# Pooled attention and two MLPs on one core: queries and keys handed over dimension first

## Chip, cores and metric

One core of a Trainium2 chip runs the whole program. The metric is the device time in microseconds from launch to end; the kernel before has a median of 672.22 us over three runs (671.64 to 672.84).

## What is computed

The inputs q, k and v have shape (2, 8, 1152, 64): 2 batches, 8 heads, 1152 positions, 64 dimensions, in float32. Queries are averaged two by two, so that each head has 576 pooled queries.

```python
q_pool = q.reshape(B, H, S // 2, 2, D).mean(axis=3)
scores = scale * np.matmul(q_pool, k.transpose(0, 1, 3, 2))
scores = scores - np.max(scores, axis=-1, keepdims=True)
attn = np.exp(scores)
attn = attn / (np.sum(attn, axis=-1, keepdims=True) + 1e-09)
x = np.matmul(attn, v)
```

The result, as 1152 rows of 512, goes through two MLPs of width 2048: `leaky(x @ w_in) @ w_out`, then the same with silu.

## The kernel before, in words

`attention()` (L287) works on 8 pairs of heads, `mlps()` (L908) follows with no attention work left. Only the attention changes.

TensorE multiplies in the type fp32r, which keeps fewer bits than float32. So every query and key operand is split into a high part (the value copied to fp32r) and a low part (value minus high part). Per pair and head j the kernel holds `K2` (128 x 1152): the 64 dimensions of the high part on one half of the partitions and those of the low part on the other half; `QH` (128 x 576): the high part of the queries on both halves; `QL` (low part of the queries, plus one row with the negated row maximum); and `KA` (high part of the keys, plus rows of ones, which adds that maximum to the product).

A pair goes through these steps.

- **Load** (`load_kq`, L358): keys and queries come from memory with positions on the partitions: one DMA for both heads' keys, three for the queries, for pair 0 by head. All DMAs are issued by SyncE, on one queue and in the order of the program (L347).
- **Pool** (`pool_q`, L408): GpSimd adds the even and the odd queries, three instructions for a pair.
- **Prepare** (`prep`, L448): TensorE turns 128 x 128 blocks by a matmul with an identity (L435), into PSUM banks. ScalarE copies from there to the high parts (L352), VectorE subtracts to get the low parts of the keys (L531) and queries (L492), and the bank is free when all have read it. For a pair after the first that is 4 groups with 15 transposes in all, which hold one bank each. In pair 0 some low parts go by way of a staging tile to GpSimd (L502, L525). `copy_qh` copies QH to the other half by DMA, `copy_ka` (L554) fills KA from K2 by four DMAs.
- **Maxima** (`max_tile`, L562): for each of 9 blocks of queries and 3 chunks of 384 keys, one matmul (L580, L581, L584) into a bank and one VectorE maximum over it (L588). `finish_max` (L599) reduces the three and SyncE writes the negated maxima as a row into QL by small DMAs (L347, `ql<-mn`, ten for a pair).
- **Scores** (`scores`, L622): for each of 9 key blocks, head and half of the queries, two matmuls (L638) into a bank and an exponential on ScalarE into a tile `e` (L642). Ten `e` tiles go round.
- **Values and sums**: `pv` (L664) multiplies `e` by v into two banks of their own (L670), and `sum_up` (L652) adds the `e` tiles up on GpSimd (L659), 16 instructions for a pair; VectorE does it for the last pair. `sums` and `finish` (L691, L768) get the reciprocals by way of DMAs and scale the values on VectorE (L773, L777).

Six PSUM banks serve preparation, maxima and scores in turn; the tokens of L319 count them. The order of instructions on every engine is written out by `Plan` (L188): each task has an engine, an estimated duration, a due time and the tasks it follows, and the planner starts on each engine the ready task that is due first. The due times of pair p are `T0 + (p + x) * T`, with T0 = 18 and T = 30 and an x for each step from `PARAMS` (L47): loads at -1.7, preparation at -1.4 to -1.15, maxima from -0.97 to -0.2. The durations of the plan set the order alone; on the chip every engine runs its list in that order, waiting at semaphores.

In the last four pairs the first weights are loaded and unpacked as well (`weight_steps`, L869): eight pieces on ScalarE and VectorE, and of the first four pieces the low parts on GpSimd (L170).

Of the kernel before, what the change touches and what calls it, by code (L numbers as in the profile page):

```python
# [11 lines left out]
ALU = mybir.AluOpType  # L12
# [7 lines left out]
def pooled_attention_two_mlps(  # L20
# [12 lines left out]
    B, H, S, D = q.shape  # L33
# [253 lines left out]
def attention(ctx, tc, q, k, v, xh, xl, weights, end_p):  # L287

    nc = tc.nc
    B, H, S, D = q.shape  # L290
# [24 lines left out]
    ps_v = ctx.enter_context(tc.tile_pool(name="ps_v", bufs=1, space=PSUM))  # L315
# [3 lines left out]
    plan.tokens(bank=NBANK, qnat=1, knat=2, vnat=2, q2=1, ops=3, acc=2, pvs=1, v=1, r=1, raw=3, wt=P["wt"])  # L319
    plan.ring("e", NE)  # L320
    banks = list(range(NBANK))

    def bank(name):
        i = banks.pop(0)
        return ps_b.tile([128, 512], F32, tag=f"b{i}", name=name), i
# [4 lines left out]
    KE = NKT // 2 * 128  # L330

    ident = const.tile([128, 128], F32, name="ident")
# [9 lines left out]
    knat, qnat, vnat, q2, K2, QH, mx, acc, e_t, vps, pvs, rec, box = ({} for _ in range(13))  # L342
# [14 lines left out]

    def load_kq(p, due, begin):  # L358
        b, h0 = p // HP, 2 * (p % HP)

        def k_part(j):
            def go():
                if p not in knat:
                    knat[p] = nat.tile([128, 2, NKT, D], F32, tag="knat", name="knat")
                js = slice(0, 2) if j is None else slice(j, j + 1)
                hs = slice(h0 + js.start, h0 + js.stop)
                return knat[p][:, js], k[b, hs].rearrange("j (p t) d -> p j t d", p=128)
            return go

        def q_part(j):  # L370
            def go():
                if p not in qnat:
                    qnat[p] = nat.tile([128, 2, 2 * (NFULL + 1), D], F32, tag="qnat", name="qnat", bufs=1)
                t = qnat[p]
                if j == 2:
                    return t[0:HALF, :, 2 * NFULL:, :], q[b, h0:h0 + 2, 2 * NFC:, :].rearrange("j (p r) d -> p j r d", p=HALF)
                return (
                    t[:, j, 0:2 * NFULL, :].rearrange("p (t r) d -> p t (r d)", r=2),
                    q[b, h0 + j, 0:2 * NFC, :].rearrange("(t p r) d -> p t (r d)", p=128, r=2),
                )  # L380
            return go

        made = {}
        if p == 0:
            made["k", 0] = dma(due, k_part(0), take=("knat",), lag=2.5)
            made["q", 0] = dma(due, q_part(0), order=[made["k", 0]], take=("qnat",), lag=2.5)
            made["q", 2] = dma(due, q_part(2), order=[made["q", 0]], lag=2.5)
            made["k", 1] = dma(due, k_part(1), order=[made["q", 2]], lag=3.0, begin=3.0)
            made["q", 1] = dma(due, q_part(1), order=[made["k", 1]], lag=3.0, begin=3.5)
        else:  # L390
            made["k", 0] = made["k", 1] = dma(due, k_part(None), take=("knat",), lag=5.0, begin=begin)
            made["q", 0] = dma(due + 0.1, q_part(0), take=("qnat",), lag=5.0, begin=begin)
            made["q", 1] = dma(due + 0.1, q_part(1), order=[made["q", 0]], lag=5.0)
            made["q", 2] = dma(due + 0.1, q_part(2), order=[made["q", 1]], lag=5.0)
        return made
# [12 lines left out]
    def pool_q(p, loads, due):  # L408
        def tail():
            q2[p] = nat.tile([128, NFULL + 1, 2, D], F32, tag="q2", name="q2", bufs=1)  # L410
# [841 lines left out]
```

## Time and profile before

| | us |
|---|---|
| median of three runs | 672.22 |
| the profiled execution | 673.36 |
| its span, first to last instruction | 670.6 |
| TensorE busy | 653.0 (97%) |
| VectorE busy | 456.1 (68%) |
| GpSimd busy | 385.3 (57%) |
| ScalarE busy | 322.7 (48%) |

The profiled execution takes 2.8 us more than its span. Busy times are sums of the durations of instructions; matmuls overlap one another, so TensorE's share says only that it seldom stood still. In the rows below PE is TensorE, PEld its weight load, DVE is VectorE, ACT ScalarE, POOL GpSimd, SPq the queue of SyncE.

### The profile page before, as it was taken

How to read it: one execution, taken by the hardware profiler on the slowest of the kernel's cores; microseconds unless marked ns; L12 is line 12 of the kernel's file. 1: busy time of each engine (PE TensorE's matmuls, PEld its weight loads, DVE VectorE, ACT ScalarE, POOL GpSimd, SP SyncE). 2: the span in 40 equal slices, each digit the busy share in tenths (PEclk: the TensorE clock that was granted, in tenths of full speed). 3: DMA queues.
4: the chain of work that ended last, by engine and by line, in shares of the span. 5: the costliest groups of instructions: out<-in, count | busy, mean ns of one | idle time of the engine just before them, and what ended most of it. 6: DMA issues, size and time to landing. Idle time of an engine off the chain costs nothing.

```text
span 670.6 us, 10322 instructions
## 1 busy us (share of the span) xinstructions
PE 653.0 (97%) x3741; PEld 530.1 (79%) x3741; DVE 456.1 (68%) x700; ACT 322.7 (48%) x694; POOL 385.3 (57%) x294
## 2 busy tenths in 40 slices
PE   6899999998999999999999999999999999999997
PEld 4566677675666666888988988999988888888986
DVE  6776768586878775885576676698988888522222
ACT  5446566584857466554443343345446543322110
POOL 7576978878797851665354354376756454522120
PEclk9799999998999999999999999999999999999999
DMA  5555151537364320033222232222233322000012
GB/s 143 142 102 146 37 142 38 143 92 199 80 193 99 104 64 20 31 127 95 95 94 95 95 95 94 95 69 89 94 95 109 111 95 95 0 1 1 1 47 94
DMA packets 41897, 59.71 MB, mean 89 GB/s; under 512 B 15324, under 2 KB 24568, under 8 KB 41848
## 3 DMA queue, kind: packets, MB, share of 16 engines
q1 hardware_dynamic: 41848, 59.07, 30.4%
q8 instruction: 29, 0.48, 0.3%
q14 instruction: 20, 0.16, 0.1%
HBM read 49.81 MB, written 2.42 MB: 78 GB/s over the span
## 4 chain that ended last, share of the span: by engine, by line
PE 87%; DVE 6%; DMA 3%; ACT 1%; issue 1%; SPq 1%; POOL 0%; DVEq 0%; ACTq 0%
PE ph L1046 30%; PE po L1117 15%; PE pf L1166 15%; PE pss L638 10%; PE pv L670 10%; PE pmx L584 4%; DVE mx L588 3%; PE prep L435 2%; DMA d<-sum 1%; DVE ql L492 1%; DMA r<-d 1%; DMA cmp<-d 1%; DMA qnat<-in_q_dram 1%; ACT qh L352 1%; SPq L347 1%
## 5 line engine op out<-in xcount | busy, mean ns | idle before, releaser
L1099 POOL TENSOR_TENSOR gl<-a,gh 128x512 fp32r<-128x512 f32 (+1 forms) x64 | 97.2, 1519 | 142.7 <-ACT gh L1093 76.1
L659 POOL TENSOR_TENSOR acc<-acc,e 128x576 f32<-128x576 f32 x98 | 140.3, 1452 | 31.0 <-ACT e L642 29.6
L642 ACT ACTIVATE e<-pss 128x288 f32<-128x288 f32 x288 | 101.4, 411 | 80.1 <-PE pss L638 73.2
L588 DVE TENSOR_REDUCE mx<-pmx 128x1 f32<-128x384 f32 x216 | 110.9, 551 | 34.4 <-PE pmx L584 29.0
L1046 PE MATMUL ph<-xh,w0h 128*128 128x320 f32 (+1 forms) x384 | 109.0, 338 | 0.5 <-ACT pvs L684 0.5
L1046 PE MATMUL ph<-xh,w0l 128*128 128x320 f32 (+1 forms) x384 | 108.7, 337 | 0.0
L1046 PE MATMUL ph<-xl,w0h 128*128 128x320 f32 (+1 forms) x384 | 108.6, 337 | 0.0
L638 PE MATMUL pss<-qh,k 128*128 128x288 f32 x288 | 88.1, 322 | 3.9 <-DVE mx L588 3.8
L670 PE MATMUL pv<-e,vnat 128*64 128x288 f32 x576 | 86.5, 422 | 0.0
L638 PE MATMUL pss<-ql,ka 128*128 128x288 f32 x288 | 81.4, 298 | 0.9 <-DMA ql<-mn 0.9
L638 PEld LDWEIGHTS pss<-qh,k 128*128 128x128 f32 x288 | 55.0, 191 | 25.2 <-DVE mx L588 10.8
L135 DVE TENSOR_SCALAR wt<-wt 128x512 f32<-128x512 f32 x56 | 40.4, 722 | 49.6 <-ACT wt L131 49.6
L1046 PEld LDWEIGHTS ph<-xh,w0h 128*128 128x128 f32 x384 | 67.7, 188 | 8.2 <-ACT pvs L684 1.0
L1046 PEld LDWEIGHTS ph<-xh,w0l 128*128 128x128 f32 x384 | 66.9, 188 | 5.6
L1046 PEld LDWEIGHTS ph<-xl,w0h 128*128 128x128 f32 x384 | 66.9, 188 | 5.0
L584 PE MATMUL pmx<-k,qh 128*128 128x384 f32 x192 | 65.4, 385 | 2.1 <-ACT e L642 1.0
L170 POOL TENSOR_TENSOR w1l<-wt,w1h 128x512 fp32r<-128x512 f32 x32 | 44.4, 1397 | 39.8 <-ACT w1h L166 39.8
L139 DVE TENSOR_SCALAR wt<-wt 128x512 uint32<-128x512 uint32 x56 | 57.9, 1033 | 1.7
L170 POOL TENSOR_TENSOR w0l<-wt,w0h 128x512 fp32r<-128x512 f32 x32 | 44.7, 1397 | 24.7 <-ACT w0h L166 24.7
L670 PEld LDWEIGHTS pv<-e,vnat 128*64 128x64 f32 x576 | 35.4, 137 | 28.9 <-issue 13.5
L1166 PE MATMUL pf<-w1h,gl 128*128 128x512 f32 x144 | 56.2, 390 | 0.0
L1166 PE MATMUL pf<-w1l,gh 128*128 128x512 f32 x144 | 56.1, 390 | 0.0
(85 smaller groups left out, 1127.6 us busy)
## 6 DMA issues: line engine op xcount, KB each, us to landing
wraw<-in_moe_w_in_dram SPq DMA_DIRECT2D x32, 512.0 KB, 3.6
wraw<-in_moe_w_out_dram SPq DMA_DIRECT2D x32, 512.0 KB, 3.1
vnat<-in_v_dram SPq DMA_DIRECT2D x8, 576.0 KB, 5.5
qnat<-in_q_dram SPq DMA_DIRECT2D x16, 256.0 KB, 5.1
knat<-in_k_dram SPq DMA_DIRECT2D x7, 576.0 KB, 5.3
ka<-k SPq DMA_DIRECT2D x16, 160.0 KB, 2.5
out_dram<-acc SPq DMA_DIRECT2D x9, 256.0 KB, 2.0
ka<-k SPq DMA_DIRECT2D x16, 128.0 KB, 2.4
```

The lines of the kernel that those rows point to most:

```text
L139: nc.vector.tensor_scalar(out=t, in0=t, scalar1=4, scalar2=1, op0=ALU.logical_shift_left, op1=ALU.logical_shift_right)
L170: self.nc.gpsimd.tensor_tensor(out=lo, in0=tf, in1=hi, op=ALU.subtract)
L584: nc.tensor.matmul(out=ps[:, 0:KC], lhsT=QH[p, j][:, t * 128:(t + 1) * 128], rhs=K2[p, j][:, ks], start=True, stop=True)
L588: nc.vector.tensor_reduce(out=mx[p][:, n:n + 1], in_=ps[:, 0:KC], op=ALU.max, axis=AX.X)
L638: nc.tensor.matmul(out=ps[:, 0:C], lhsT=lhsT[:, ks], rhs=rhs[:, cs], start=not last, stop=last)
L642: nc.scalar.activation(out=e_t[p, j, t][:, cs], in_=ps[:, 0:C], func=ACTF.Exp, scale=scale)
L659: e.tensor_tensor(out=acc[p, j], in0=e_t[p, j, 0] if t == 1 else acc[p, j], in1=e_t[p, j, t], op=ALU.add)
L670: nc.tensor.matmul(out=vps[p, c][own[j], 0:C], lhsT=vnat[p][:, j, t, :], rhs=e_t[p, j, t][:, c * C:(c + 1) * C], start=(t == 0), stop=(t = ...
L1046: nc.tensor.matmul(out=box[x][:, c, 0:n], lhsT=wt[:, kk, fs], rhs=m[:, kk, chunk(g, c)], start=(kk == 0 and wt is wh and m is xh), stop=(k ...
L1099: nc.gpsimd.tensor_tensor(out=gl, in0=box["a", x], in1=gh, op=ALU.subtract)
L1117: nc.tensor.matmul(out=box[x][:, c, 0:n], lhsT=wt[:, f, ms], rhs=y[:, c * n:(c + 1) * n], start=(f == 0 and wt is oh and y is gh), stop=(f ...
L1166: nc.tensor.matmul(out=box[x][:, 0, :], lhsT=y[:, ts], rhs=wt[:, f, :], start=(f == 0 and y is gh and wt is oh), stop=(f == FB - 1 and y i ...
```

## The change

The function `kernel()` hands q and k over in another order: k as (batch, head, dimension, position), q as (batch, head, dimension, even or odd, position); the position order of the keys within a head changes with it. A head's 64 dimensions then land on 64 partitions, and two heads fill 128. The transposes, `ident`, the staging tiles and `copy_qh` go.

For pairs 2 to 7 `prep` works on both heads at once, from SBUF to SBUF: one pooling add on GpSimd (128 x 576), two high copies on ScalarE (128 x 1152 and 128 x 576), two low subtractions on VectorE (the same shapes). Ten DMAs then put the halves into K2 (four), QH (four) and QL (two), each between 64 partitions and 64 partitions. KA takes two DMAs. For pair 1 the loads go into four `e` tiles, its low parts are made on GpSimd, and it is due much earlier. Pair 0 is prepared by head with no matmul (`prep_first`).

All eight PSUM banks become one tile, `psum`. Pair 0's maxima take three banks at a time: 3 matmuls of up to 512 columns (6 for the shared block), one VectorE maximum over 1152 columns straight into the negated row, in two sets of three banks. The first three key blocks of its first head use the two banks of the values meanwhile. The planner's T0 is 16 and T is 27.

```diff
 PARAMS = dict(
-    t0=18.0,
-    t=30.0,
+    t0=16.0,
+    t=27.0,
...
-    prep1=(20.0, 22.0, 24.0, 26.0),
+    prep1=(10.0, 11.0, 12.0, 13.0),
...
-    low_pool=((0, 0, 1), (0, 1, 0), (0, 1, 1)),
-    ql_pool=(0, 1),
+    k_pool=((1, 1), (0, 1)),
...
-    load1=12.0,
+    load1=4.0,
...
-    plan.tokens(bank=NBANK, qnat=1, knat=2, vnat=2, q2=1, ops=3, ...)
+    plan.tokens(bank=0, trio=2, early=2,  qnat=1, knat=1, vnat=2, kf=1, ops=3, ...)
+    banks, trios, early = [], [0, 3], [NBANK, NBANK + 1]
+    psum = ps_b.tile([128, NBANK + 2, 512], F32, name="psum")
...
+    def prep_first(p, j, loads, out):
...
+            hi = add("ACT", w, d + 0.1 * i, lambda cs=cs: copy("ACT", K2[p, j][own[j], cs], knat[p][own[j], cs]), after=[loads["k", j]])
+            def low(e, cs=cs):
+                e.tensor_tensor(out=K2[p, j][oth[j], cs], in0=knat[p][own[j], cs], in1=K2[p, j][own[j], cs], op=ALU.subtract)
...
+    def prep(p, loads, due, out):
+        halves = p == 1
+        def pooled():
+            operands(p)
+            even, odd = qnat[p] if halves else [qnat[p][:, r] for r in range(2)]
+            q2[p], qf[p] = even, odd.bitcast(F32R)
+            nc.gpsimd.tensor_tensor(out=even, in0=even, in1=odd, op=ALU.add)
...
+        low = nc.gpsimd if halves else nc.vector
+        def q_lo():
+            low.tensor_tensor(out=q2[p].bitcast(F32R), in0=q2[p], in1=qf[p], op=ALU.subtract)
...
+                low.tensor_tensor(out=x.bitcast(F32R), in0=x, in1=kf[p][:, cols[i]], op=ALU.subtract)
...
+        x = add("POOL", 1.45, due[0], pooled, after=loads["q"], take=("ops",))
...
+            kh.append(add("ACT", 0.21 + 0.84 / n, due[1], k_hi(i), after=[loads["k"][i], x], order=kh[-1:], take=take))
+            kl.append(add(eng, 1.95 * w / n, due[1], k_lo(i), after=kh[-1:]))
+        qh = add("ACT", 0.63, due[0], q_hi, after=[x])
+        ql = add(eng, w, due[2], q_lo, after=[qh])
+        for j in range(2):
+            d = due[2] + 0.2 * j
+            a = move(lambda j=j: kf[p][own[j]], lambda j=j: K2[p, j][own[j]], kh, d)
+            bs = [
+                move(lambda j=j, i=i: keys(i)[own[j]].bitcast(F32R), lambda j=j, i=i: K2[p, j][oth[j], cols[i]], [kl[i]], d)
+                for i in range(n)
+            ]
+            cs = [move(lambda j=j: qf[p][own[j]], lambda j=j, r=r: QH[p, j][r], [qh], d) for r in own]
+            e = move(lambda j=j: q2[p][own[j]].bitcast(F32R), lambda j=j: QL[p % 3, j][own[j]], [ql], due[3])
...
+    def max_unit(u2, out, due, after):
...
+            for c in range(0, S, 512):
...
+                    nc.tensor.matmul(out=ps[0:rows, ks], lhsT=QH[p, h][:, cs], rhs=K2[p, h][:, ks], start=True, stop=True)
+        def dve():
...
+            nc.vector.tensor_reduce(out=max_row(p, j)[:, u:u + 1], in_=ps[:, 0:S], op=ALU.max, axis=AX.X, negate=True)
...
+def layout(name, a):
+    if name in ("q", "k"):
+        b, h, s, d = a.shape
+        rows = (128, s // 128) if name == "k" else (s // 2, 2)
+        a = a.reshape(b, h, *rows, d).transpose(0, 1, 4, 3, 2)
+        a = a.reshape(b, h, d, s) if name == "k" else a
+    return a
```

## Rows read from the trace of the kernel before

**Rows 1.** Stretches: bounds, length, busy of PE, PEld, DVE, ACT, POOL; PEclk, DMA share, GB/s.

```profile
22.00:32.00 10.00, 7.94 (x37) 6.51 (x37) 6.07 (x16) 7.34 (x19) 4.65 (x5) 0.75 0.30 70
...
114.50:144.00 29.50, 29.45 (x200) 20.69 (x199) 21.03 (x44) 19.06 (x51) 24.89 (x19) 1.00 0.46 119
144.00:173.00 29.00, 27.30 (x171) 18.00 (x168) 20.62 (x39) 17.55 (x46) 22.93 (x18) 0.94 0.49 130
173.00:204.00 31.00, 29.45 (x194) 20.25 (x195) 25.85 (x52) 21.59 (x56) 26.63 (x21) 1.00 0.53 147
...
265.00:446.00 181.00, 180.88 (x1016) 163.98 (x1017) 125.05 (x150) 80.63 (x141) 94.78 (x66) 1.00 0.27 88
```

**Rows 2.** The page's part 4: shares by line of the chain that ended last.

```profile
PE ph L1046 30%; PE po L1117 15%; PE pf L1166 15%; PE pss L638 10%; PE pv L670 10%; PE pmx L584 4%; DVE mx L588 3%; PE prep L435 2%; DMA d<-sum 1%; DVE ql L492 1%; DMA r<-d 1%; DMA cmp<-d 1%; DMA qnat<-in_q_dram 1%; ACT qh L352 1%; SPq L347 1%
```

**Rows 3.** Timeline of TensorE around a group of transposes: start, length, instruction.

```profile
114.28 0.29 PE L638 MATMUL pss<-ql,ka 128*128 128x288 f32 x1
114.41 0.60 PE L435 MATMUL prep<-ident,knat 128*128 128x128 f32 x4
114.76 0.38 PE L638 MATMUL pss<-qh,k 128*128 128x288 f32 x1
114.98 0.29 PE L638 MATMUL pss<-ql,ka 128*128 128x288 f32 x1
```

**Rows 4.** Timeline of the first 32 us; brackets: idle time before, and what ended it.

```profile
3.81 1.09 PE L435 MATMUL prep<-ident,knat 128*128 128x128 f32 x4 [3.81 <-DMA knat<-in_k_dram]
...
10.17 1.49 DVE L588 TENSOR_REDUCE mx<-pmx 128x1 f32<-128x384 f32 x3 [0.78 <-PE pmx L584]
...
23.04 1.02 DVE L588 TENSOR_REDUCE mx<-pmx 128x1 f32<-128x384 f32 x2
...
29.26 0.37 PE L638 MATMUL pss<-ql,ka 128*128 128x288 f32 x1 [0.86 <-DMA ql<-mn]
...
31.24 0.44 PE L584 MATMUL pmx<-k,qh 128*128 128x384 f32 x1 [1.01 <-ACT e L642]
```

**Rows 5.** Groups by line and shape: busy us, mean ns | idle before, releasers.

```profile
L588 DVE TENSOR_REDUCE mx<-pmx 128x1 f32<-128x384 f32 x216 | 110.9, 551 | 34.4 <-PE pmx L584 29.0 <-PE pmx L581 2.2
L531 DVE TENSOR_TENSOR k<-prep,k 64x512 fp32r<-64x512 f32 x29 | 20.0, 689 | 7.0 <-ACT k L352 6.2 <-ACT low L352 0.2
...
L492 DVE TENSOR_TENSOR ql<-prep,qh 64x512 fp32r<-64x512 f32 x14 | 9.6, 688 | 5.2 <-ACT qh L352 2.6 <-PE prep L435 2.4
L659 DVE TENSOR_TENSOR acc<-acc,e 128x576 f32<-128x576 f32 x14 | 10.2, 755 | 5.7 <-ACT e L642 5.7
L412 POOL TENSOR_TENSOR q<-qnat 64x128 f32<-64x128 f32 x8 | 3.6, 452 | 5.5 <-DMA qnat<-in_q_dram 5.5
L417 POOL TENSOR_TENSOR q<-qnat 128x256 f32<-128x256 f32 x15 | 10.8, 733 | 0.1
```

**Rows 6.** The running sums on GpSimd, instructions of line 659: ns min/median/max.

```profile
L659 POOL TENSOR_TENSOR acc<-acc,e x98: 1394/1417/2312, 27.3 to 242.6; 128x576 f32<-128x576 f32 x98
```

**Rows 7.** Timeline: a running sum on GpSimd, and an instruction of VectorE beside it.

```profile
137.21 2.25 POOL L659 TENSOR_TENSOR acc<-acc,e 128x576 f32<-128x576 f32 x1 [0.34 <-ACT e L642]
137.44 0.74 DVE L773 TENSOR_TENSOR pvs<-pvs,r 128x576 f32<-128x576 f32 x1
```

**Rows 8.** Stretches of 1 us in which KA copies (121) and loads (127) fill the DMA engines.

```profile
121.00:122.00 1.00, 1.00 (x12) 0.43 (x11) 0.56 (x1) 0.75 (x4) 0.31 (x1) 1.00 1.03 226
...
127.00:128.00 1.00, 1.00 (x8) 0.96 (x9) 0.56 (x1) 0.38 (x2) 1.00 (x1) 1.00 1.01 364
```

**Rows 9.** Issues on SyncE's queue in one pair period: start, time taken, transfer, count.

```profile
120.73 0.58 SPq L347 DMA_DIRECT2D knat<-in_k_dram  x1
...
134.44 2.52 SPq L347 DMA_DIRECT2D ql<-mn  x4
...
144.80 2.44 SPq L347 DMA_DIRECT2D ql<-mn  x4
...
150.38 0.58 SPq L347 DMA_DIRECT2D knat<-in_k_dram  x1
```

More of the change, by code (lines that the diff above doesn't have):

```diff
@@ L426, in pool_q @@
-        add("-", 0.0, due, after=list(out.values()), give=("qnat",))
-        return out
-    def transpose(ps, c, src):
-        n, m = src.shape
-        nc.tensor.transpose(out=ps[0:m, c:c + n], in_=src, identity=ident[0:n, 0:n])
-    def key_cols(t):
-        c = t // 2 * 128 + (KE if t % 2 or t == NKT - 1 else 0)
-        return slice(c, c + 128)
-    def k_nat(p, j, t):
-        return knat[p][:, j, t:t + 2, :].rearrange("p t d -> p (t d)")
-    def q_nat(p, i, heads):
-        rows = q2[p][0:128 if i < NFULL else HALF, i]
-        return rows[:, 0, :] if heads == (0,) else rows.rearrange("p j d -> p (j d)")
@@ L548, in copy_qh @@
[L548 to L558 removed]
+                if i == 0:
+                    kf[p] = nat.tile([128, S], F32R, tag="kf", name="kf", bufs=1)
@@ new lines, in prep @@
+        for name, ts in users.items():
+            give = (name,) if name == "kf" or not halves else tuple(("e", "half", name[0], i) for i in range(2))
+            add("-", 0.0, 0.0, after=ts, give=give)
+    def copy_ka(p, j, out, due, after):
+        if p == 0:
+            parts = (slice(0, 512), slice(512, S))
+            for i, cs in enumerate(parts):
+                go = lambda cs=cs: (KA[p % 2, j][own[j], cs].bitcast(F32), K2[p, j][own[j], cs].bitcast(F32))
+                out["ka", j, i] = [dma(due, go, after=out["kh", j, i] + after, lag=3.0)]
+        else:
+            go = lambda: (KA[p % 2, j][own[j]].bitcast(F32), K2[p, j][own[j]].bitcast(F32))
+            out["ka", j, 0] = out["ka", j, 1] = [dma(due, go, after=out["kh", j, 0] + after, lag=3.0)]
@@ L566, in max_tile @@
         for j in (0, 1) if u == NFULL else (0,) if u < NFULL else (1,):
[L567 to L572 removed]
+            x = u if u <= NFULL else u - NFULL - 1
+            deps += out["qu", j][0 if x < 2 else 1]
+            deps += out["k", j, 0 if c == 0 else 1]
         def pe():
@@ L622, in scores @@
     def scores(p, t, j, out, due, before):
-        ks = key_cols(t)
-        x = 2 * KE if t == NKT - 1 else ks.start // KE * KE
-        deps = out["kh", j, x] + out["kl", j, x] + out["ka", j, 1 if x else 0] + out["mr", j]
-        for full in (True, False):
-            deps = deps + out["qh", j, full] + out["ql", j, full]
+        ks = slice(t * 128, (t + 1) * 128)
+        i = int(t >= 4)
+        deps = out["k", j, i] + out["ka", j, i] + out["mr", j] + out["qh", j] + out["ql", j]
         exps = []
+        first = p == 0 and j == 0 and t < P["lead"]
+        store = early if first else banks
         for c in range(2):
@@ L642, in act @@
                 nc.scalar.activation(out=e_t[p, j, t][:, cs], in_=ps[:, 0:C], func=ACTF.Exp, scale=scale)
-                banks.append(i)
+                store.append(i)
             token = (("e", p, t, j),) if c == 0 else ()
-            before = add("PE", 0.265, due, pe, after=deps, order=[before] if before else [], take=("bank",) + token)
-            exps.append(add("ACT", 0.42, due, act, after=[before], order=exps[-1:], give=("bank",)))
+            before = add("PE", 0.265, due, pe, after=deps, order=[before] if before else [], take=("early" if first else "bank",) + token)
+            exps.append(add("ACT", 0.42, due, act, after=[before], order=exps[-1:], give=("early" if first else "bank",)))
         return exps, before
@@ L852, in attention @@
                 av[t, j] = sum_up(p, t, j, ex[t, j] + [av[t - 1, j]], [], due + 2.0)
+        if p == 0:
+            add("-", 0.0, 0.0, after=[x for t in range(P["lead"]) for x in ex[t, 0]], give=("v",))
         last = []
```

325 lines of the change are left out of this document (147 added, 178 removed).

## The prediction

> **What bounds the kernel now.** I read the stretches first, since the shares of the whole span mix three stages. In a full pair of heads TensorE is busy for 29.45 of 29.5 us, VectorE for 21.03, ScalarE for 19.06, GpSimd for 24.89 [rows 1]. So TensorE sets the pace there, and GpSimd comes next with 4.6 us to spare. When the first weights are unpacked as well it is less clean: 1.7 us idle and a granted clock of 0.94 in the stretch from 144, 1.55 us idle in the one from 173 [rows 1]. From 265 on the MLPs keep TensorE busy for 180.88 of 181 us [rows 1], and their instructions don't change, so what the attention saves arrives at the end.
>
> The chain of work that ended last says the same by lines: scores and values have 10% each, the transposes (`prep`, L435) 2%, which is 13.4 us of 670.6 [rows 2]. Then I read the timeline for the price of one group of transposes, and the first 32 us for what the start waits for. There VectorE's maxima are the bound: they run from 10.17 to 24.06, TensorE waits at 29.26 for a row of maxima, and pair 1's first maximum comes at 31.24 [rows 4].
>
> **Transposes away (pairs 2 to 7).** A group of four begins at 114.41 and the next score matmul at 114.76. The one after that comes at 114.98, 0.22 later, where scores otherwise follow one another by 0.13 (114.28 to 114.41) [rows 3]. So the group costs 0.35 + 0.09 = 0.44 us, 0.11 for a transpose. Fifteen in a pair and six pairs give 90 x 0.11 = 9.9 us, all on the path, as TensorE is never idle beside them. The other bound is the chain's 13.4 us, which holds the transposes of pairs 0 and 1 too. A group of three costs about as much as one of four, so I take 10.5 us, or 1.75 a pair. A full pair would take 27.75 us.
>
> **VectorE and ScalarE.** A pair loses six subtractions of 64 x 512 at 0.69 us, 4.1 us without the small ones, and gains two of 128 x 1152 and 128 x 576 from SBUF. The second is of the kind of the running sum on VectorE, 0.755 us; from 512 to 576 columns the price grows by 1.03 ns a column (0.689 to 0.755) [rows 5], so the first costs 0.755 + 576 x 1.03 ns = 1.35. That is 2.1 for 4.1 us. ScalarE loses copies too. Neither sets the pace, so both count nothing; they stay covered as long as VectorE has less than 27 us in a pair, and it had 25.85 in the fullest stretch of 31 [rows 1].
>
> **GpSimd.** Three adds (0.452 + 2 x 0.733) go, one of 128 x 576 comes, which I price as a running sum, 1.42 [rows 5, 6]: 0.5 us less. But the two new subtractions read both operands from SBUF. Beside such an instruction of 0.74 us a running sum took 2.25 instead of 1.42 us [rows 6, 7]. If each delays GpSimd by its full length, it has 24.89 - 0.5 + 2.1 = 26.5 us of work in a pair of 27.75. That is covered; in the stretch with weights 26.63 - 0.5 + 2.1 = 28.2 is not, by 0.5 us, for some two pairs. I take +1 us; the ends are 0 and 6 x 2.1 = +12.6.
>
> The Trainium skill ("SBUF — State Buffer", Who interferes with whom) says that a VectorE instruction with two SBUF inputs and a GpSimd instruction that reads SBUF exclude each other for the whole instruction. The trace agrees in the one row above. By that rule today's two scalings of 0.755 count fully as well: 16 x 1.42 + 1.42 + 2.1 + 1.5 = 27.7 us in a pair, no slack at all, and with the weights some 3 us over; the sum would be 660 rather than 657.5.
>
> **DMAs.** A pair has 10 halves to move where it had 2, but two KA copies and one query load instead of four and three: some 30 for 26 issues at 0.6 us [rows 9], 18 us of SyncE in 27.75. The halves are 4 x 295 KB and 6 x 147 KB, 2.06 MB. Copies between 64 partitions ran at 226 GB/s with all DMA engines busy, where loads had 364 [rows 8], so they fill the queue for 9.1 us. What is late next is the operands of the next pair. Today its load is issued at 120.73, and the last rows of the pair before it, which end that pair's maxima, at 144.8, 24 us later [rows 9]; 22.7 at the new pace. The new path: loads are still moving 7.3 us after the issue [rows 8, 9]; up to 1.4 behind a running sum and 1.4 for the add; about 2 for ScalarE; 1.35 for VectorE; then the first head's five moves, half of 9.1, and some 2 to land. That makes 20 us, inside 22.7. Second-head maxima come 15 x 0.55 us later [rows 5]. Rows of maxima queue behind the moves on SyncE, but those issued at 134 to 137 are not needed before the ones at 144.8. I count nothing; the ends are 0 and some 4 us a pair.
>
> **Pair 0 and 1.** The keys landed at 3.81 [rows 4] and will about then. VectorE has two key subtractions, two adds and two copies of 64 x 256 to 640 before the maxima, 3.3 us by the line through [rows 5] (0.16 us + 1.03 ns a column), so its first maximum can start near 8 instead of 10.17. A maximum over 1152 columns costs 0.551 + 768 x 1.03 ns = 1.34 us; nine take 12.1, against 13.9 from 10.17 to 24.06. They end near 21 with the instructions between them. Today the wait for the last row ends 5.2 us after the last maximum; with fewer DMAs between I take 3, so the second head's scores start near 24 instead of 29.26. The transposes of pair 1 that TensorE did before then are gone, and pair 1's operands come from GpSimd, which has little else before the first running sums at 27.3 [rows 6]. I take 5 us. The ends are 2 (rows as late as today) and 8: up to 3 us more if TensorE gets its full clock in the stretch from 22, granted 0.75 with 7.94 us busy [rows 1].
>
> **Sum.** -10.5 - 5 + 1 = -14.5 us on an execution of 673.36. The median of the runs is 1.1 us below that one: 672.2 - 14.5 = 657.7, so I say 657.5.
>
> **Rivals.**
>
> *More than the sum.* Preparation held a PSUM bank for each of four groups; without it maxima and scores have six banks to themselves. If that ends the idle time and the clock loss after 144 (1.7 + 1.55 us, and 0.06 of 29) [rows 1] and the start gains its 8 us, it is -10.5 - 8 - 5 = -23.5, or 649. For it: those losses lie where VectorE is fullest. Against: the weights stay and the pair gets shorter. Chance 0.2.
>
> *GpSimd sets the pace.* Its work of 26.5 us leaves 1.25 idle, and it idles 4.6 now. If half of that is waiting for the exponentials at the start of a pair and stays, a pair takes 28.8 and saves 0.7: -4.2 - 5 = -9, or 663. For it: the row of 2.25 us. Against: ten `e` tiles let GpSimd lag behind. Chance 0.2.
>
> *TensorE was not the bound*, so that only the start gains: 667. Against it stands 29.45 of 29.5. Chance 0.04.
>
> *Late halves, slower.* The planner lets TensorE begin a pair's maxima as early as its estimates allow, and TensorE runs in order: where the moves land later than planned, scores and values behind the first maximum wait too, once in each of six pairs. Slack is 2.7 us by my path. From 14.5 / 6 = 2.4 us of waiting in a pair the gain is gone; 4 us in each would give 672.2 - 14.5 + 24 = 682. For it: the moves need 9.1 us of the queue. Against: the pace of today leaves 24 us. Chance 0.06, and 0.04 that the wait just cancels the gain.
>
> **Numbers.** The forecast has 0.46; its own ends are 652 to 661. The range of 646 to 667 takes in most of the first two rivals and leaves out the others, 0.14, and some of the edges. A measurement of this kernel tells 0.2%, 1.3 us, from no change. Faster: 0.46 + 0.2 + 0.2 + 0.04 = 0.90; within: 0.04; slower: 0.06.
>
> **What would show it.** No line of `prep` matmuls; pair periods (from key load to key load) near 28 instead of 29.7; GpSimd near 26 us busy in each, running sums over 2 us more often; nine maxima of about 1.34 us that end near 21; the second head's scores near 24; first MLP matmul near 250 instead of 265. I am wrong if TensorE idles before the first maximum of each pair (late halves), if GpSimd is busy all through a pair, or if the MLPs take other than 405 us.

## The result, and the profile after

The changed kernel takes **682.11 us** (median, 681.14 to 683.39) against 672.01 for the kernel before in the same comparison: a ratio of **1.015, 95% interval 1.0126 to 1.0173**. The forecast was 657.5 and "faster". One execution of the run x1 below, the profiled one, took 1235.74 us with TensorE at its lower level of 1.2 GHz throughout (a matmul of 288 columns every 0.24 us, where [rows 3] have 0.13), so nothing is read from the profile of x1 but the order of its instructions.

The stretches of the changed kernel, with the columns of [rows 1]: the whole attention, the ten microseconds of the start, four pairs, 2 to 5 (each from about its first score matmul to the next pair's), and the same length of MLP.

```profile
0.00:275.70 275.70, 246.68 (x1448) 164.65 (x1448) 176.13 (x303) 140.70 (x357) 199.40 (x146) 0.95 0.60 151
...
22.00:32.00 10.00, 6.66 (x27) 5.45 (x26) 2.38 (x2) 3.94 (x11) 2.90 (x3) 0.80 0.82 177
84.90:116.70 31.80, 29.30 (x185) 19.37 (x183) 20.18 (x34) 16.21 (x42) 27.05 (x18) 1.00 0.60 156
116.70:152.10 35.40, 31.03 (x184) 21.13 (x182) 17.57 (x34) 16.78 (x42) 26.44 (x19) 0.90 0.64 160
152.10:186.80 34.70, 31.21 (x185) 20.98 (x183) 22.79 (x42) 18.57 (x46) 25.55 (x19) 0.90 0.72 186
186.80:222.90 36.10, 33.30 (x196) 21.91 (x194) 23.64 (x45) 19.57 (x49) 29.98 (x22) 0.91 0.61 154
...
275.70:456.70 181.00, 180.97 (x1016) 164.06 (x1017) 124.96 (x150) 80.64 (x141) 94.73 (x66) 1.00 0.27 88
```

The attention of the kernel before, in the same columns, and its pairs 2 to 4:

```profile
0.00:265.10 265.10, 251.61 (x1573) 171.54 (x1573) 195.08 (x387) 160.82 (x422) 192.43 (x162) 0.98 0.42 110
...
87.70:117.10 29.40, 29.40 (x199) 20.70 (x197) 21.03 (x43) 18.91 (x51) 24.63 (x20) 1.00 0.41 103
117.10:146.60 29.50, 29.45 (x200) 20.68 (x198) 20.73 (x43) 19.06 (x51) 24.95 (x20) 1.00 0.46 119
146.60:180.50 33.90, 31.84 (x199) 21.20 (x197) 25.49 (x51) 20.46 (x54) 25.59 (x21) 0.95 0.51 136
```

The MLPs take 405 us in both kernels, so the whole loss, 275.7 - 265.1 = 10.6 us, lies in the attention. It splits into three parts.

- **Idle**: TensorE stands still for 275.7 - 246.7 = 29.0 us, before for 265.1 - 251.6 = 13.5: +15.5. Some 5 of them fall in the first 12.4 us, where no transposes run any more and the time is set by the maxima.
- **Clock**: the column of the granted clock can't be taken as it is. It shows 1.00 from 0 to 24.5 us too, but there the matmuls run at the lower level, 288 columns in 0.24 us and not in 0.13 as in [rows 3]:

```profile
23.37 0.44 PE L661 MATMUL psum<-qh,k 128*128 128x288 f32 x1
23.61 0.44 PE L661 MATMUL psum<-ql,ka 128*128 128x288 f32 x1
```

In the kernel before this first stretch ends at 13.4 (384 columns in 0.32 us up to there, in 0.17 behind it). With it TensorE is busy at the lower level for 38.1 us of the attention, before for 18.1. Half of that is the loss, as an estimate: 19.0 and 9.1 us, +10.0.

- **Work**: what is left of the busy time is 227.6 us, before 242.5: -14.9. As an estimate, to some 3 us: w1, x2 and f1 below have the same matmuls but for one and come to 227 to 230.

The 125 transposes are gone, and at the forecast's 0.11 us each that is 13.8 us, so they were worth about what it said. But TensorE now waits in each of the four pairs shown, for 2.5 to 4.4 us (before for nothing in pairs 2 and 3 and 2.1 in pair 4), and the granted clock is down to 0.90 or 0.91 over three of these pairs: in each of the three TensorE goes on at the lower level after it has stood still, for 6.8 us from 144, 178 and 212.

From a pair's first score matmul to the next pair's, pairs 1 to 6 take 26.4, 31.8, 35.4, 34.7, 36.3 and 28.4 us, before 30.7, 29.4, 29.4, 34.0, 32.2 and 28.7. So up to pair 2's scores the changed kernel is 2.8 us ahead (84.94 against 87.74), in pairs 2 to 5 it loses 13.2, and behind them the two take the same time to 0.2 us.

The chain of waits, by engine and by line, answers to [rows 2]:

```profile
PE 80%; DMA 9%; DVE 7%; SPq 2%; issue 1%; ACT 1%; POOL 0%; DVEq 0%; POOLq 0%; ACTq 0%
PE ph L1058 30%; PE po L1129 15%; PE pf L1178 14%; PE psum L661 8%; PE psum L693 7%; DMA r<-d 3%; DVE mx L582 3%; PE psum L578 3%; SPq L343 2%; DMA ql<-mn 2%; DMA d<-sum 2%; PE psum L602 1%; DVE pvs L796 1%; DMA qnat<-in_q_dram 1%; DVE mn L607 1%
```

The kernel before has PE 87%, DMA 3%, SPq 1%. DMA goes from some 20 to 61 us of the chain. The transfers named are not the new halves: they are the reciprocal's trip (row sums to DRAM as `d<-sum`, spread out as `cmp<-d`, inverted on VectorE, back as `d<-cmp`, broadcast as `r<-d`), the rows of maxima (`ql<-mn`) and a load of queries. The chain in one pair of the changed kernel (start, length, what):

```profile
192.08 5.91 DMA d<-sum
197.99 0.02 issue
198.01 1.53 DMA cmp<-d
...
199.70 0.95 DVE mx L582 x2
200.65 0.61 DVE knat L505
...
206.56 4.64 DMA r<-d
...
211.30 0.76 DVE pvs L796
212.06 0.48 DVE mx L582
212.53 0.04 issue
212.58 0.85 PE psum L661 x2
```

VectorE stands at the reciprocal until the trip's first legs have landed, then at the normalisation until `r` has landed, and only then takes the maximum behind it, for which TensorE waits (9.1 us in four such waits, before 3.8 in seven). The start, with the columns of [rows 4]:

```profile
9.33 1.36 DVE L607 TENSOR_REDUCE mn<-psum 128x1 fp32r<-128x1152 f32 x1 [0.91 <-PE psum L602]
9.42 2.76 POOL L437 TENSOR_TENSOR k<-knat,k 64x512 fp32r<-64x512 f32 x2
10.72 1.64 DVE L350 CAST qh<-qh 64x320 fp32r<-64x320 f32 x1
...
12.42 7.59 PE L602 MATMUL psum<-k,qh 128*128 128x512 f32 x18 [2.06 <-DVE qh L350]
...
21.76 2.62 DVE L607 TENSOR_REDUCE mn<-psum 128x1 fp32r<-128x1152 f32 x2 [0.16 <-PE psum L602]
...
29.86 0.61 PE L661 MATMUL psum<-ql,ka 128*128 128x288 f32 x1 [2.16 <-DMA ql<-mn]
```

A maximum takes 1.36 us, as forecast. But TensorE and the maxima wait until 12.4 for one VectorE copy of 64 x 320, which takes 1.64 us beside the second of two subtractions on GpSimd (10.65 to 12.18). The keys land at 4.5 us (before 3.8), the maxima end at 24.38 (before 24.06) and the second head's scores begin at 29.86 (before 29.26).

The groups of the new instructions, with the columns of [rows 5], and the running sums as in [rows 6]:

```profile
L607 DVE TENSOR_REDUCE mn<-psum 128x1 fp32r<-128x1152 f32 x9 | 12.0, 1355 | 2.2 <-PE psum L602 2.1
L505 DVE TENSOR_TENSOR knat<-knat,kf 128x1152 fp32r<-128x1152 f32 x6 | 11.0, 1834 | 1.0 <-POOL acc L682 1.0
...
L500 DVE TENSOR_TENSOR qnat<-qnat 128x576 fp32r<-128x576 f32 x6 | 7.2, 1208 | 2.6 <-ACT qnat L348 2.3 <-DMA ql<-mn 0.3
```

```profile
L682 POOL TENSOR_TENSOR acc<-acc,e x98: 1391/1419/2533, 27.1 to 252.7; 128x576 f32<-128x576 f32 x98
```

And one pair period of SyncE's queue, with the columns of [rows 9]:

```profile
151.64 0.59 SPq L343 DMA_DIRECT2D knat<-in_k_dram  x1
...
157.38 0.54 SPq L343 DMA_DIRECT2D d<-sum  x1
161.45 0.33 SPq L343 DMA_DIRECT2D cmp<-d  x1
...
171.40 0.62 SPq L343 DMA_DIRECT2D k<-knat  x1
172.12 4.97 SPq L343 DMA_DIRECT2D ql<-mn  x6
...
181.95 2.42 SPq L343 DMA_DIRECT2D ql<-mn  x4
184.42 0.59 SPq L343 DMA_DIRECT2D knat<-in_k_dram  x1
```

SyncE issues in order: from 157.92 to 161.45 it does nothing until `d<-sum` has landed, with the halves behind it; six rows of maxima stand behind the halves. Such standing is not new, though. SyncE's longest waits for the trip, before and after (total, times, longest):

```profile
SPq L347 <- DMA d<-sum: 20.7, 7, 4.0
SPq L347 <- DVE cmp L733: 16.9, 7, 4.1
...
SPq L343 <- DMA d<-sum: 25.4, 7, 5.8
SPq L343 <- DVE cmp L756: 10.6, 4, 3.6
```

With `d<-cmp` (2.5 and 4.3 us) that makes 40 us in either kernel. What has grown is the time to landing: the median of `r<-d`, 144 KB in both, went from 3.3 to 4.7 us, that of the rows of 0.5 KB from 2.0 to 2.4. VectorE's waits for `cmp` and `r` went from 8.4 to 18.7 us.

### The profile page after: what moved, and what is told of

Its sections match the earlier page's. It is cut to its first block, busy times and chain, and to the rows that moved or that the text cites. A ratio compares the mean times of both kernels' runs of the same rounds, so it can differ in the third digit from the quotient of the medians.

```text
span 680.9 us, 9990 instructions
## 1 busy us (share of the span) xinstructions
PE 648.1 (95%) x3616; PEld 523.2 (77%) x3616; DVE 437.0 (64%) x616; ACT 302.6 (44%) x629; POOL 392.3 (58%) x278
## 3 DMA queue, kind: packets, MB, share of 16 engines
q1 hardware_dynamic: 36200, 71.46, 37.7%
## 4 chain that ended last, share of the span: by engine, by line
PE 80%; DMA 9%; DVE 7%; SPq 2%; issue 1%; ACT 1%; POOL 0%; DVEq 0%; POOLq 0%; ACTq 0%
PE ph L1058 30%; PE po L1129 15%; PE pf L1178 14%; PE psum L661 8%; PE psum L693 7%; DMA r<-d 3%; DVE mx L582 3%; PE psum L578 3%; SPq L343 2%; DMA ql<-mn 2%; DMA d<-sum 2%; PE psum L602 1%; DVE pvs L796 1%; DMA qnat<-in_q_dram 1%; DVE mn L607 1%
## 5 line engine op out<-in xcount | busy, mean ns | idle before, releaser
L682 POOL TENSOR_TENSOR acc<-acc,e 128x576 f32<-128x576 f32 x98 | 147.5, 1533 | 24.0 <-ACT e L665 23.7
L665 ACT ACTIVATE e<-psum 128x288 f32<-128x288 f32 x288 | 102.5, 411 | 97.1 <-PE psum L661 81.7
L582 DVE TENSOR_REDUCE mx<-psum 128x1 f32<-128x384 f32 x189 | 93.9, 547 | 59.4 <-PE psum L578 56.2
L661 PE MATMUL psum<-qh,k 128*128 128x288 f32 x288 | 93.5, 339 | 9.8 <-DVE mx L582 9.1
L661 PE MATMUL psum<-ql,ka 128*128 128x288 f32 x288 | 85.1, 310 | 4.7 <-DMA ql<-mn 3.8
L693 PE MATMUL psum<-e,vnat 128*64 128x288 f32 x576 | 89.3, 434 | 0.0
L661 PEld LDWEIGHTS psum<-qh,k 128*128 128x128 f32 x288 | 57.8, 201 | 38.6 <-DVE mx L582 13.9
L661 PEld LDWEIGHTS psum<-ql,ka 128*128 128x128 f32 x288 | 58.4, 203 | 5.6 <-DMA ql<-mn 4.4
L693 PEld LDWEIGHTS psum<-e,vnat 128*64 128x64 f32 x576 | 36.2, 140 | 29.8 <-issue 16.0
```

The costliest lines, as they stand in the source:

```text
L582: nc.vector.tensor_reduce(out=mx[p][:, n:n + 1], in_=ps[:, 0:KC], op=ALU.max, axis=AX.X)
L661: nc.tensor.matmul(out=ps[:, 0:C], lhsT=lhsT[:, ks], rhs=rhs[:, cs], start=not last, stop=last)
L665: nc.scalar.activation(out=e_t[p, j, t][:, cs], in_=ps[:, 0:C], func=ACTF.Exp, scale=scale)
L682: e.tensor_tensor(out=acc[p, j], in0=e_t[p, j, 0] if t == 1 else acc[p, j], in1=e_t[p, j, t], op=ALU.add)
L693: nc.tensor.matmul(out=vps[p, c][own[j], 0:C], lhsT=vnat[p][:, j, t, :], rhs=e_t[p, j, t][:, c * C:(c + 1) * C], start=(t == 0), stop=(t = ...
```

## The experiments

Ratios are to the kernel before, on the same chip and in the same comparison. Differences between two runs are of their medians; by their ratios they come out up to 3 us larger or smaller.

### The plan: due times, landing times, pair 1

```diff
 a1:  -    t0=16.0, t=27.0,      +    t0=18.0, t=30.0,
 a3:  -    return dma(d, go, after=after, lag=3.0)
      +    return dma(d, go, after=after, lag=5.0)      # loads 7.0, trip 5.0, 3.0, 6.0
 a4:  -    prep1=(10.0, 11.0, 12.0, 13.0), load1=4.0,
      +    prep1=(20.0, 22.0, 24.0, 26.0), load1=12.0,
```

> The changed kernel with the planner's old pace, T0 = 18 and T = 30, nothing else. Three theories of the loss of 10 us: Queue (the ten halves and the loads stand ahead of small transfers on the one queue, these land later than the planner thinks, and VectorE waits in order), Pace (the due times are now closer together than the chip can follow), Lock (VectorE's new subtractions and GpSimd's sums shut each other out). Pace: 672 or less, with even pair periods. Queue: the halves stay, but the order of the instructions has more room, 675 to 682. Lock: the work is the same, 680 to 684.

> The changed kernel with longer landing times in the planner alone: halves 5 us instead of 3, loads 7 instead of 5, sum to memory 5 instead of 2.2, back 3, broadcast of r 6 instead of 3. No transfer changes, only the order of instructions around the waits. Queue, with the planner's too short times as the way in which it costs: VectorE's and GpSimd's waits for DMAs (13.7 + 5.0 + 5.3 us) fall to under 10 and the kernel takes 668 to 677. If the late landings cost by the bytes themselves, or by Lock: 679 to 685.

> The changed kernel with pair 1 loaded and prepared as late as before (due 12 and 20 to 26 instead of 4 and 10 to 13). If the early halves of pair 1 hold up the rows of pair 0's second head (the last row landed at 29.8, 5.4 us after the last maximum), the second head's scores start 2 to 3 us earlier, but pair 1's maxima later: 679 to 683. If the early preparation is worth what it is meant to be: 684 to 690.

Measured: 692.71 us (ratio 1.0282, 1.0259 to 1.0305), 689.80 (1.0255, 1.0219 to 1.029) and 702.26 (1.0422, 1.037 to 1.0475). All three are slower than the change as it is. The old due times don't bring the old time back, landing times nearer to the trace don't either, and the early pair 1 is worth some 20 us, not a cost.

a1 and a3 change nothing but the order of the instructions, and that alone costs 10.6 and 7.7 us, as much as the loss to be explained. a3 tells more: told the later landings, the planner moves VectorE's late steps back, and VectorE's waits for `cmp` and `r` fall from 18.7 to 1.7 us. The time rises all the same, since TensorE now waits for halves and for rows of maxima:

```profile
PE psum L578 <- DMA k<-knat: 7.4, 2, 5.7
PE psum L661 <- DMA ql<-mn: 6.1, 5, 2.1
```

### The halves

```diff
 a2:  -    return dma(d, go, after=after, lag=3.0)
      +    return dma(d, go, after=after, lag=3.0, queue="ACT")
 c1:  +    kl = add("DVE", 1.4, ..., out=K2[p, j][oth[j]], in0=knat[p][own[j]], in1=K2[p, j][own[j]])
      +    up = add("ACT", 0.63, ..., copy("ACT", QH[p, j][oth[j]], q2[p][own[j]]))
 c2:  c1 and t0=18.0, t=30.0
 d1:  +    return dma(d, go, after=[dma(d, go, after=after, lag=0.0)], lag=3.0)
```

> The changed kernel with the halves (K2, QH, QL) issued from ScalarE's queue instead of SyncE's. Queue: the reciprocals' transfers no longer stand behind them, VectorE's wait for r at its scaling falls from 13.7 us to under 4, and the kernel takes 664 to 674. Pace and Lock: the bytes and the order of VectorE stay, 679 to 684; if the 16 DMA engines and not the queue are what is shared, also 679 to 684, with as long a landing of r.

> The changed kernel in which, for pairs 2 to 7, the ten halves don't go by DMA: ScalarE writes the high parts and VectorE the low parts by head straight into K2, QH and QL, 64 partitions at a time (twice as many of VectorE's subtractions from SBUF: 4.2 us a pair instead of 2.1, six copies on ScalarE instead of two). Halves (the 2 MB a pair that go by DMA, and make the other transfers late on which VectorE and TensorE wait): 655 to 668, with r landing in about 3 us again. Lock (VectorE's subtractions from SBUF against GpSimd's sums): there are twice as many, so 685 to 695. If both engines are merely in a bad order: 675 to 685.

> The same as the run before with the planner's old pace, T0 = 18 and T = 30. Halves: also fast, 658 to 672; the pace of the planner then matters by a few us. If the gain of the run before hangs on one lucky order, this one is 10 us or more from it.

> The changed kernel with every half sent twice (the same transfer again right behind the first, the use after the second): 2 MB and 10 issues more in a pair, all else as it is but for what the planner makes of the later issue. Halves: 695 or more. Lock or another cause on the engines: 682 to 688.

Measured: a2 694.69 us (1.0309, 1.028 to 1.0339), c1 685.05 (1.0188, 1.0154 to 1.0223), c2 680.59 (1.0111, 1.008 to 1.0142), d1 869.72 (1.2921, 1.2881 to 1.296).

From ScalarE's queue the halves are worse, because ScalarE stands at them with its exponentials behind (waits of ScalarE in a2: total, times, longest):

```profile
ACT e L666 <- DMA qh<-e: 13.4, 1, 13.4
...
ACT e L666 <- DMA k<-kf: 7.6, 1, 7.6
```

Without halves (c1) the queue moves 59.07 MB as before the change, in place of 71.46, and nothing is gained. That is no clean acquittal: each head's subtraction now costs VectorE about as much as both together did,

```profile
L518 DVE TENSOR_TENSOR k<-knat,k 64x1152 fp32r<-64x1152 f32 x12 | 21.9, 1827 | 0.5
```

and VectorE waits 20.8 us for the trip's `cmp`, 10.1 at the longest. So c1 and c2 show that the halves need not be there for the loss, not that they have no part in it. In d1 the second copy of a half waits for the first to land, so SyncE stands at it, 42.2 us at `qh<-qnat`, 42.0 at `k<-knat`, 34.7 at `k<-kf` and 21.2 at `ql<-qnat`; the halves land later as well, and the run can't tell the two apart, nor say anything on bytes.

### The start

```diff
 h1:  -            if j == 0:
      +            if j == 2:
                       up = add("DVE", ..., copy("DVE", QH[p, j][oth[j], cs], ...))
                   else:
                       up = add("ACT", ..., copy("ACT", QH[p, j][oth[j], cs], ...))
```

> The changed kernel in which ScalarE instead of VectorE makes pair 0's first head's second copy of QH (two casts, which took 0.81 and 1.64 us beside GpSimd's subtractions, the second with VectorE and TensorE waiting behind it until 12.4). The maxima then run without that gap and end near 22.5 instead of 24.4; if the start of the second head's scores follows from it, the kernel takes 679 to 681; if that start is set by the rows queued behind pair 1's halves, no change, 682.

Measured: 676.70 us (1.0051, 1.0026 to 1.0076), 5.4 less than the change as it is. The maxima begin at 8.72, run with gaps of 0.2 to 1.2 us and end at 22.09:

```profile
8.72 2.62 DVE L607 TENSOR_REDUCE mn<-psum 128x1 fp32r<-128x1152 f32 x2 [0.53 <-PE psum L602]
...
18.20 3.89 DVE L607 TENSOR_REDUCE mn<-psum 128x1 fp32r<-128x1152 f32 x3 [1.18 <-PE psum L602]
```

Pair 1's scores begin at 53.99 in place of 58.49. The gain that the forecast gave the start was there; the two copies of this head on the wrong engine took it. (The order of the later instructions changes with them.) TensorE also comes to its higher level sooner, at 19.2 in place of 24.5 us.

### VectorE against GpSimd

```diff
 l1:  -    low.tensor_tensor(out=..., in0=q2[p], in1=qf[p], op=ALU.subtract)
      +    nc.vector.memset(q2[p], 0.0)        # and for the keys, pairs 2 to 7
 g1:  h1 and
      -    dve_add=(),
      +    dve_add=((4, 1), (7, 1)),
```

> The changed kernel with VectorE's 12 subtractions of k's and q's low rows in pairs 2 to 7 replaced by memsets of the same shape (the low parts of those pairs are left out of the computation): one write and no read from two SBUF tensors. Lock theory: GpSimd's sums come back from 1533 to 1417 ns (98 of them, 11 us) and the rows are ready earlier; 660 to 668 us. Chain theory: the trip is as late as before, 676 to 682. Ring theory: the sums are faster and the ring comes free earlier, 665 to 675.

> The changed kernel with pair 0's second copy of q on ScalarE (which alone gave 676.7) and two of the sixteen running sums of each pair moved from GpSimd to VectorE (0.75 us each there). Ring theory: GpSimd goes from 26 busy us in a pair to 23, ScalarE's wait for a free exponential tile falls from 9 to under 3 us, 668 to 672 us. Chain theory: VectorE has 1.5 us more in each pair ahead of its late steps; 677 to 682. Lock theory: fewer sums to hold up, 672 to 676.

Measured: l1 681.27 us (1.0135, 1.0082 to 1.0188), g1 681.07 (1.011, 1.0059 to 1.0161). In l1 the sums come down to

```profile
L688 POOL TENSOR_TENSOR acc<-acc,e 128x576 f32<-128x576 f32 x98 | 138.4, 1438 | 29.3 <-ACT e L671 28.8
```

from a mean of 1533 ns (1452 before the change). So the two engines did hold each other up, by 9 us of GpSimd's time in all, and giving that back is worth nothing. The Trainium skill ("SBUF — State Buffer", Who interferes with whom) says that a VectorE instruction with two SBUF inputs and a GpSimd instruction that reads SBUF contend; the 1533 and 1438 ns agree, and the time doesn't follow. l1 runs its instructions in the very order of the change, so Lock falls as the cause. In g1 GpSimd has two sums a pair less, but ScalarE still waits 10.9 us for it, as in h1, so the wait that Ring names was not made shorter; the kernel is 4.4 us slower than h1, and TensorE waits 6.0 us for halves (`k<-knat`, twice). What speaks against Ring is w1 below: the same wait of 11.0 us at 667.2.

### The reciprocal's trip

```diff
 w1, w2 (the changed kernel, the kernel before):
      -    x = dma(due, down, after=[x])
...
      -    return [y, dma(due, lambda: up2(1), after=[x], order=[y], lag=3.0)]
      +    rec[p] = one_r
      +    return [x]
 x1:  -    return box["d2", p], box["cmp", p]
      +    return box["d2", p], one_c
      -    x = add("DVE", 0.21, due, lambda: nc.vector.reciprocal(...), after=[x])
      +    rec[p] = one_r          # r<-d goes to another tile
 x2:  x1 and
      -    return box["d", p], box["sum", p][0:128:32, :]
      +    return box["d", p], one_r[0:128:32, 0, :]     # cmp<-d and r<-d read d0 and d20, written once
 e1:  h1 and
      -    x = dma(due, down, after=[x])
      +    x = dma(due, down, after=[x], lag=4.5)        # up 3.2, up2 5.5
```

> The changed kernel without the reciprocal's trip: the row sums stay on TensorE and ScalarE, but their five transfers and VectorE's reciprocal go, and the tile of reciprocals holds ones (the normalisation of pairs 0 to 6 is left out of the computation). Chain theory: the loss of 10.6 us sits where VectorE stands in its order at the reciprocal and at the normalisation (23 us of waits for r, cmp and d in the changed kernel, 8 in the kernel before) and TensorE behind it; then this kernel takes 655 to 665 us against 682 and the same cut in the kernel before gains 8 us or less. Lock theory: the late rows of q and k come from GpSimd and VectorE holding each other up; the trip is beside it, and this kernel takes 675 to 682. Ring theory: ScalarE waits for a free exponential tile that GpSimd's sums still hold (9.2 us against 0.9); also 675 to 682.

> The same cut in the kernel before (the normalisation of pairs 0 to 6 is left out), as the control. Chain theory: 664 to 670 us, since there VectorE waits 8 us for the trip and TensorE has its transposes to do meanwhile. Lock and Ring theories: 670 to 673. If both kernels lose the same, the trip has no part in the difference between them.

> The changed kernel with the reciprocal's five transfers a pair still made, at the same places of the queue, but read by nobody: the second leg sends a tile of ones, and VectorE multiplies by a tile of ones and makes no reciprocal (the normalisation of pairs 0 to 6 is left out of the computation). Without trip and reciprocal the kernel took 667 us. Wait theory: what costs is VectorE standing in its order until the trip has landed; 665 to 671 us. Traffic theory: what costs is the trip's five issues and 0.6 MB a pair on the queue, ahead of rows and loads; 677 to 683 us.

> As the unread trip (683.7 us), with the same five transfers at the same places of the queue, but each sends something that is there from the start (a tile of ones, two DRAM tiles written once), so that SyncE never waits in its order for a leg to land or for ScalarE's sums (the normalisation of pairs 0 to 6 is left out of the computation). Order theory: what the trip costs is SyncE standing in its order at the legs (40 us a run in the changed kernel), with the halves, rows and loads of the next pair behind it; 664 to 672 us. Traffic theory: the transfers themselves; 680 to 685.

> The changed kernel with pair 0's second copy of q on ScalarE (which alone gave 676.7) and the planner told the landing times that the trace shows for the trip alone (4.5, 3.2 and 5.5 us in place of 2.2, 2.2 and 3.0), so that VectorE's reciprocal and normalisation stand later in its order. Wait theory: VectorE's waits for cmp and r fall from 15 to under 5 us and the kernel takes 665 to 672. If a late step only makes something else late (the PV tile is single, the row sums' tile too): 675 to 682.

Measured: w1 **667.2** us (0.9885, 0.9824 to 0.9946), w2 670.49 (0.996, 0.9938 to 0.9982), x1 **683.7** (1.0148, 1.0112 to 1.0185), x2 682.51 (1.0145, 1.0089 to 1.02), e1 685.0 (1.0161, 1.0122 to 1.02).

Without the trip the changed kernel gains 15 us and is faster than before; the kernel before gains 1.6 from the same cut. So what was cut separates the two kernels. (The five transfers are 0.31 MB a pair, 71.46 MB in all against 69.29 in w1, half of what x1's expectation says.) But neither of the two waits that the chain suggested turns out as the price of it, as far as runs in different orders can tell.

- **VectorE's wait.** By its edit x1 has no wait for the trip, and its time is that of the change as it is. In e1 the waits for `cmp` and `r` fall from 13.1 (h1) to 5.7 us, and the time rises by 8: TensorE now waits 13.5 us for rows of maxima, in h1 2.2. a3 said the same.
- **SyncE's standing.** x1 and x2 run the same instructions in the same order on every engine; x2 alone has no waits for the trip on SyncE, and its ratio is that of x1 (1.0145 and 1.0148).

The attention of w1 and then of x2:

```profile
0.00:261.90 261.90, 239.63 (x1449) 160.58 (x1449) 176.65 (x297) 138.99 (x357) 199.38 (x146) 0.97 0.59 151
```

```profile
0.00:270.70 270.70, 243.45 (x1448) 162.36 (x1448) 182.45 (x298) 139.38 (x356) 202.78 (x146) 0.99 0.61 154
```

TensorE is idle for 22.3 and 27.3 us: even with no trip there are 9 us more idle than before the change. (These are the slowest of w1's four executions, 662.18 to 669.11 us, and the fastest of x2's, 678.01 to 686.63, so they lie 9 us apart and the medians 15.) The chain of x2 shows what stands in the place of the trip's waits (three pieces of it):

```profile
141.73 5.49 DMA wraw<-in_moe_w_in_dram
...
185.27 8.64 DMA wraw<-in_moe_w_out_dram
...
215.41 5.11 DMA ql<-mn
```

Loads of weights and rows of maxima, on the same queue. Where one transfer was let off, another one bound. x2 takes 128.5 us for pairs 2 to 5, where the change takes 138.2, and gives 4.9 of that back in pairs 6 and 7.

**What stays open**: x1, x2 and w1 hold the queue's order of the change, the trip aside, only for its first 69 transfers, up to pair 2; behind that the planner lays out other orders, since tasks are missing, and that of w1 is not that of x2. w1 and x2 differ in the five transfers of a pair and in the order, and the runs don't tell which of the two makes the 15 us. a1, a3 and e1 show that another order alone can move the time by 8 to 11.

### Towards a version that beats both

```diff
 e3:  h1 and
      -    x = dma(due, up, after=[x])
      -    x = add("DVE", 0.21, due, lambda: nc.vector.reciprocal(out=box["cmp", p], ...), after=[x])
      -    x = dma(due, down2, after=[x], lag=3.0)
      +    x = add("DVE", 1.92, due, lambda: nc.vector.reciprocal(out=box["sum", p], ...), after=[x])
      +    x = dma(due, down, after=[x], lag=3.0)
 e4:  e3 and lag=5.5 for r<-d
 f1:  e4 and queue="ACT" for the trip's three transfers, lag=5.0 for d<-sum
```

> The changed kernel with pair 0's second copy on ScalarE and a shorter trip: VectorE takes the reciprocal of the row sums where they stand (128x288, 1.92 us by the last pair's row, in place of 0.21), and two of the three legs go; the wait for cmp goes with them. Wait theory: the wait for cmp (13 us on VectorE in the kernel with only the copy moved) is gone, 12 us of VectorE's work come in seven pairs where it has 5 us a pair to spare; 667 to 673. If VectorE's work decides instead: 677 to 684.

> As the short trip, with the planner told 5.5 us in place of 3.0 for the landing of the reciprocals' broadcast. Wait theory: the wait for r goes too; 664 to 671, at or under the short trip. If a late normalisation holds the single PV tile: above the short trip, 673 to 680.

> The changed kernel with pair 0's second copy on ScalarE, the short trip, and the trip's three transfers issued from ScalarE's queue, planned with 5.0 and 5.5 us to landing. With SyncE the same trip took 672.1 us. Order theory: SyncE no longer stands at the trip (34 us a run with the short trip there), ScalarE has idle time to stand in; 660 to 669, faster than both kernels. Traffic theory: 670 to 674. If ScalarE's stream stands at the legs instead, with the exponentials behind it: 675 to 690, as when the halves were issued there.

Measured: e3 675.63 us (1.0038, 1.0017 to 1.0059), **e4 672.09** (0.9976, 0.9955 to 0.9997), **f1 671.82** (0.9988, 0.9954 to 1.0022). With one copy moved and a trip of three transfers in place of five, the change is level with the kernel before; e4's interval lies just under 1, by about as much as can be told from no change. f1's attention:

```profile
0.00:265.50 265.50, 241.67 (x1449) 162.97 (x1449) 194.78 (x301) 140.70 (x359) 202.90 (x146) 0.98 0.61 156
```

It ends at 265.5 (before 265.1): 10 us less busy time, 10 us more idle. SyncE hardly stands at the trip any more (6 us, in e4 34), and that brings nothing beyond e4, which agrees with x2.

## Why the prediction was wrong

**What failed, in short.** Two steps: "all on the path, as TensorE is never idle beside them", and with it the nothing that I put for the DMAs. The transposes' work went as forecast, but TensorE stands still for 15.5 us more and loses 10.0 more to the lower level of the clock, while in pairs 2 to 5 it waits for transfers of the one queue or for VectorE behind them. A third step, the start, was mis-sized: -5 became +1.5 at pair 1's scores.

**Transposes: right.** Forecast -10.5 us of TensorE's work for pairs 2 to 7, with pairs 0 and 1 some 13.8 by the same price; measured -14.9, an estimate to some 3 us. The price of 0.11 us from [rows 3] held.

**Pair 0 and 1: the step failed.** The maxima cost 1.355 us (forecast 1.34), but they began at 9.33 instead of 8 and ended at 24.38 instead of 21. The keys landed 0.7 us later than before, which I had not reckoned with. I had priced the two copies of 64 x 256 to 640 by VectorE's line and had not asked what runs on GpSimd beside them, nor that TensorE's second block needs one of them: it took 1.64 us where that line gives 0.16 + 320 x 1.03 ns = 0.49. The second head's scores began 0.6 us later than before and pair 1's 1.5 later (58.49 against 57.01), where I had taken 5 off. h1 gave 5.4 back. The Trainium skill ("SBUF — State Buffer", Who interferes with whom) says that a copy or cast on VectorE can take the port shared with GpSimd as well, and that the one issued second stands still for the whole of the other's instruction. The trace agrees: GpSimd's subtraction runs from 10.65 to 12.18, the copy begins at 10.72 and ends at 12.36, just behind it. I had applied that section to the subtractions alone.

**VectorE and GpSimd: sizes wrong, conclusion right.** The subtractions took 1.83 and 1.21 us, not 1.35 and 0.755; the running sums cost 98 x 0.081 = 7.9 us more (1533 against 1452 ns). l1 shows that none of this is on the path, so the +1 was 0.

**DMAs, counted at nothing: the step that failed.** I followed one path only, the operands of the next pair, and found 20 us of work inside 22.7. That path was longer than said: the load is issued at 151.64 and the last half at 171.40, with its landing still to come (a median of 4.9 us for `k<-knat`). What I left out were the other passengers of the same queue: the trip's legs, the rows, the query load (one of 6.8 us on the chain). That the transposes had covered these landings is likely but not shown. The cut of the trip out of both kernels (15 us and 1.6) shows that its price lies here, and leaves open whether by its transfers or by the order that goes with them. The bound of 4 us a pair and the miss of 24.6, 3.1 for each of eight pairs, agree in number alone, since 6.5 of the 24.6 belong to the start.

**The sum: the assumption under it failed.** "All on the path, as TensorE is never idle beside them" was read from the kernel before. It says that TensorE was the bound then; it does not say how close the next bound was. A stretch with 29.45 of 29.5 busy has no waits in which to read that, and GpSimd's 24.89 was the only second bound to which I gave a price.

**Rivals.** "Late halves" gave 682 us, the number that came, and that is luck: it placed the wait before the first maximum of each pair, and in the changed kernel it isn't there. It is the next thing behind, though: TensorE waits 7.4 us for halves in a3 and 6.0 in g1. "GpSimd sets the pace" had the wrong engine: l1 gave GpSimd 9 us back and the kernel nothing. "TensorE was not the bound" had 0.04 and was nearest in kind. The signs that I named for being wrong (idle before the first maximum, GpSimd busy throughout, MLPs other than 405 us) all stayed away, while the kernel was slower.

**Clock.** I had gaining clock at the start as one end of a range and losing it nowhere. TensorE came to its higher level at 24.5 in place of 13.4 us and fell from it four times (before twice), three of these in waits. So 15.5 us more of waiting came with 10.0 us of clock, and the 14.9 us of work saved did not make up for them.

## What to carry to other kernels

Work taken off an engine that is busy 99.8% of the time is worth its price only down to the next bound: before counting it, list for one period every in-order queue that feeds the engine and how late each of its results already is, small transfers too. A fully busy engine hides these lags from the profile; cutting a suspect out of both kernels (15 us here, 1.6 there) points at them. Removing one wait that the chain names need not shorten anything where another transfer of the same queue lands little earlier. And where a planner lays out the order, a cut changes the order too: compare two runs of one order, as x1 with x2 and l1 with the change, before a difference is put down to the cut.

## What the runs showed of the hardware that was not expected

- A VectorE copy of 64 x 320 took 1.64 us beside a subtraction on GpSimd and one of 64 x 256 0.81, though a copy has one input only. Each ended 0.15 to 0.2 us behind the GpSimd instruction that had begun before it.
- VectorE's subtraction over 64 partitions takes as long as over 128: 1.83 us for 1152 columns in either shape.
- A reciprocal on VectorE takes 1.92 us for 128 x 288 in the last pair, against 0.69 for a subtraction of 512 columns [rows 5]. Seven more of them in place of two DMA legs a pair (e3, e4) were no loss: 675.63 and 672.09 us against 676.70 in h1.
- Landing times on the one queue spread widely: on the changed kernel's chain `r<-d` took 3.0 to 6.8 us and `d<-sum` 4.5 and 5.9, and a row of maxima of 0.5 KB or less took 5.1 us in x2.
